# A hand-written order of 821 operations, written anew from the first product to the last chunk but one: linear attention into a SiLU layer on one Trainium2 core

## The chip, the cores and the metric

The kernel runs on one core of a Trainium2 chip. The core has TensorE (matrix products, in the profile PE, and PEld for its weight loads), VectorE (DVE), ScalarE (ACT), GpSimd (POOL) and SyncE (SP); 16 DMA engines move data between the device memory and the core's SBUF. Products land in PSUM, which has 8 banks. The metric is the device time of one execution in microseconds.

## The reference

Inputs `q`, `k`, `v` are 8 batches x 8 heads x 576 rows x 64; the two weight matrices are 512 x 2048 and 2048 x 512, all float32.

```python
q_s = exp(q - max(q, -1)); q_s /= sum(q_s, -1)          # over the 64 of a head
k_s = exp(k - max(k, 2));  k_s /= sum(k_s, 2)           # over the 576 rows
kv  = einsum('bhsd,bhse->bhde', k_s, v)                 # 64 x 64 per head
x   = einsum('bhsd,bhde->bhse', q_s, kv)                # then (4608, 512)
h   = x @ w_in
out = (h / (1 + exp(-h))) @ w_out                       # (4608, 512)
```

## The kernel before

The 4608 rows are worked as chunks 0 to 8. Chunk 0 is the 576 rows of batch 0; chunk 1 has 448 rows, chunks 2 to 8 have 512, and a chunk's rows may come from two batches. The attention of batch b is made just ahead of the chunks that need it.

The two layers of chunks 1 to 8 use a scheme with seven block products for eight (Strassen's, in Winograd's form): of rows, columns and inner dimension two halves each. It needs sums of weight blocks (once), of input blocks and of results. All names that follow are operations of the kernel; t is a chunk, b a batch, c one of two pairs of heads, i a product from 1 to 7.

- **Loads.** `lq`, `lk`, `lv` (b.c) load float32 halves of a batch, 576 KB each, into tiles with two buffers per name. Batch 0 and batches 3 to 7 are loaded by SyncE's queue, batches 1 and 2 by GpSimd's. `W1a0` to `W1d` (first layer) and `W2a` to `W2d` (second layer) are loaded by GpSimd's queue, which also turns them to float16.
- **Attention.** `eq`, `ek`: exp on ScalarE. `z`: row sums and reciprocal on VectorE. `n`: the division of q on GpSimd (line 216; batch 0 and `n1.1` on VectorE). `vc`: the cast of v to bfloat16, on GpSimd from batch 2 on (line 144). `tq`: one DMA transpose of q on SyncE's queue (line 226; batches 0 and 1 on TensorE, `tr`, with copies `tc`). `kv`, `kc`: the 64 x 64 products and their normalisation. `X`: the product that makes the layer's input, copied out of PSUM by `x` (suffix a: ScalarE, v: VectorE).
- **First layer.** Chunk 0, plainly: `w` is one block of 128 columns over 576 rows (8 matmuls of 288 columns), into one of four pairs of PSUM banks; `h` its tanh (ScalarE), `v` the product of it on VectorE. Chunk 1 does half of its columns plainly (`m`, with SiLU `mu`). The rest is done in two groups of seven products: `g t.group.i`, 8 matmuls each, lines 412 to 433. Products 1, 6, 7, 4 add up in banks 0 and 1; between them `s` copies the sum reached (to tiles h0, h1, h2), `a` adds products 2, 5, 3 to the copy (VectorE, line 403), and `u` applies SiLU (ScalarE, line 409). So product 6 must wait for the copy after product 1, product 7 for the copy after 6, and so on.
- **Second layer.** Chunk 0 plainly: `p`, with copies `po` and stores `os`. From chunk 1 on `b t.i.half` (8 matmuls, line 503), snapshots `sa`, `sb`, `sc`, sums `wa`, `wb`, `wc`, `wl` and stores `o t.half` (four DMAs on SyncE's queue). `o t.0` stores what `wa` and `wb` have filled.
- **Sums of SBUF operands on VectorE.** `WS group.i` (line 373) and `T i` (line 487) are sums of weight blocks, `xs` (line 383) of the layer's input, `S t.i` (line 477) of the first layer's results. `T1` needs the parts of the second layer's weights up to `W2b2`, `T2` all of them.
- `gcopy` copies the 64 rows of chunk 0's result that belong with chunk 1.

Nothing schedules the program. The body first writes out the head (lines 545 to 621: warm-up matmuls `heat`, batch 0's attention, the issue of the weight loads, the first halves of `w0` and `w2`). Then each operation is entered in a table under its name (lines 624 to 805), and the text `ORDER` (lines 18 to 67) lists the names; they are called in that order (lines 807 and 808), and each engine runs its own operations in the order in which they were called. Semaphores make an operation wait for the data it reads and for the buffers it overwrites, and whatever stands behind it on its engine waits with it. A DMA waits in its queue in the same way; the queue of GpSimd also holds GpSimd's operations.

Of the kernel before, what the change touches and what calls it, by code (L numbers as in the profile page):

```python
# [15 lines left out]


ORDER = """
    lk1.0 w1 lk1.1 w2 h1 w0 h2 v1 w3 h0 W2b1 w5 v0 v2 h3 w4 WS0.1 h5 w6 v3 h4 W2b2 v4 w7 v5 w8 h7 h6 v7 w9
    lv1.0 h8 v6 w11 v8 h9 lv1.1 w10 eq1.0.0 v9 h11 WS0.2 w12 eq1.1.0 v11 h10 w13 WS1.1 eq1.0.1 v10 h12 w15  # L20
    qp1a h13 v12 w14 eq1.1.1 v13 qp1b WS1.2 W2c1 p0 h14 z1.0 ek1.0 p1 z1.1.0 n1.0 z1.1.1 p2 h15 ek1.1 v15 p3
    WS1.4 W2c2 tr1.0 v14 lq2.0 p4 tc1.0a tc1.0b lq2.1 n1.1 p5 W2d p6 lk2.0 T1 vc1.0 lk2.1 p7 tr1.1 lv2.0
    vc1.1a vc1.1b gcopy WS1.3 kv1 lv2.1 tc1.1b p8 tc1.1a kc1 WS0.3 xt1.0 xt1.1 x1.0a x1.1v p9 x1.2a x1.3v
    g1.1.1 xs1.1 xs1.2 xs1.4 g1.1.2 s1.1.0a WS0.4 p10 xs1.3 eq2.0 a1.1.0 p11 eq2.1 z2.0 g1.1.6 g1.1.5
    s1.1.1a z2.1 n2.0 p12 ek2.0 g1.1.7 p13 s1.1.2v n2.1 ek2.1 p14 a1.1.2 g1.1.4 p15 tq2 u1.1.4 g1.1.3 po2v
    vc2.1 po1a m0 po3v po0a a1.1.1 u1.1.0 vc2.0 m1 lk3.0 mu0 m2 T2 lq3.0 mu1 lq3.1 m3 u1.1.2 lk3.1 T3 m4
    lv3.0 u1.1.1 lv3.1 m5 T4 mu2 os0 mu4 kv2 mu5 m6 mu3 kc2 X2.0 mu6 X2.1 x2.0v m7 x2.1a x2.3a x2.2v g2.1.1
    mu7 xs2.1 xs2.2 g2.1.2 s2.1.0v b1.1.0 ek3.0 S1.1 g2.1.6 eq3.1 lk4.0 S1.2 b1.2.0 os1 s2.1.1a b1.1.1 xs2.3
    xs2.4 eq3.0 a2.1.0 g2.1.7 vc3.0 sa1 b1.2.1 lq4.0 z3.1 s2.1.2a g2.1.5 vc3.1 ek3.1 b1.6.0 a2.1.2 n3.1
    lk4.1 g2.1.4 z3.0 g2.1.3 u2.1.0 g2.0.2 u2.1.4 wa1 n3.0 b1.6.1 a2.1.1 u2.1.2 g2.0.1 sb1 S1.3 kv3 tq3  # L30
    s2.0.0a b1.5.0 kc3 u2.1.1 S1.4 g2.0.6 b1.7.0 s2.0.1v lv4.0 ek4.1 b1.7.1 lv4.1 a2.0.0 os3 g2.0.7 sc1
    ek4.0 b1.5.1 s2.0.2v g2.0.5 eq4.0 lk5.0 wc1 lq4.1 g2.0.4 a2.0.2 os2 b1.4.0 vc4.0 lk5.1 z4.0 u2.0.4
    g2.0.3 u2.0.2 b1.3.0 lv5.0 vc4.1 a2.0.1 u2.0.0 lq5.0 b1.4.1 n4.0 X3.0 wl1v X3.1 kv4 x3.0a x3.1v x3.2a
    b1.3.1 kc4 x3.3a xs3.1 u2.0.1 g3.1.1 xs3.2 wb1 g3.1.2 s3.1.0a xs3.3 xs3.4 g3.0.2 S2.1 g3.1.6 S2.2 eq4.1
    b2.2.0 s3.1.1a b2.1.0 z4.1 ek5.0 b2.1.1 a3.1.0 g3.1.7 n4.1 sa2 ek5.1 b2.6.0 s3.1.2v g3.1.5 vc5.0 tq4
    g3.1.4 a3.1.2 u3.1.0 b2.6.1 u3.1.4 S2.3 g3.1.3 sb2 lq5.1 g3.0.1 u3.1.2 a3.1.1 lv5.1 lk6.0 b2.7.0 s3.0.0a
    o1.0 S2.4 b2.2.1 u3.1.1 a3.0.0 g3.0.6 lv6.0 b2.7.1 s3.0.1v eq5.0 g3.0.5 wa2 g3.0.7 sc2 lq6.0 z5.0 b2.4.0
    s3.0.2a lk6.1 b2.5.0 vc5.1 eq5.1 a3.0.2 g3.0.4 o1.1 n5.0 z5.1 g3.0.3 u3.0.4 b2.5.1 a3.0.1 n5.1 u3.0.0
    b2.4.1 wc2 u3.0.2 X4.0 X4.1 kv5 x4.1v x4.0a tq5 wl2v b2.3.0 u3.0.1 x4.3v g4.1.1 xs4.1 x4.2a b2.3.1 xs4.2
    s4.1.0a S3.1 g4.1.2 wb2 g4.1.6 lq6.1 a4.1.0 ek6.1 b3.1.0 xs4.3 s4.1.1a b3.1.1 xs4.4 S3.2 ek6.0 g4.1.5  # L40
    g4.1.7 sa3 eq6.0 b3.2.0 s4.1.2v eq6.1 b3.2.1 lq7.0 kc5 lk7.0 b3.6.0 a4.1.2 lv6.1 lq7.1 g4.1.4 o2.0 wa3
    g4.1.3 z6.0 u4.1.4 b3.5.0 u4.1.0 S3.3 g4.0.1 lk7.1 b3.6.1 a4.1.1 s4.0.0a g4.0.2 sb3 u4.1.1 g4.0.6 a4.0.0
    b3.5.1 s4.0.1a S3.4 b3.7.0 vc6.1 u4.1.2 g4.0.7 z6.1 vc6.0 g4.0.5 s4.0.2a b3.7.1 a4.0.2 n6.1 g4.0.4 sc3
    u4.0.2 g4.0.3 wc3 n6.0 b3.3.0 u4.0.4 a4.0.1 b3.4.0 u4.0.0 X5.0 X5.1 kv6 x5.0a x5.1v tq6 x5.3a x5.2v
    b3.3.1 u4.0.1 xs5.1 g5.1.1 xs5.2 wb3 b3.4.1 s5.1.0v o2.1 ek7.1 g5.1.2 kc6 g5.1.6 wl3a xs5.3 xs5.4 a5.1.0
    lv7.0 b4.2.0 s5.1.1a lv7.1 b4.1.0 S4.1 eq7.1 g5.1.7 ek7.0 b4.2.1 s5.1.2v o3.1 g5.1.5 S4.2 b4.1.1 u5.1.0
    a5.1.2 g5.1.4 sa4 g5.0.2 o3.0 u5.1.4 wa4 g5.1.3 S4.3 u5.1.2 vc7.1 g5.0.1 b4.6.0 a5.1.1 vc7.0 s5.0.0a
    b4.6.1 a5.0.0 u5.1.1 g5.0.6 S4.4 b4.5.0 s5.0.1a b4.5.1 sb4 u5.0.0 g5.0.7 g5.0.5 s5.0.2v b4.7.0 eq7.0
    a5.0.2 b4.7.1 z7.1 g5.0.4 sc4 g5.0.3 b4.4.0 a5.0.1 u5.0.4 b4.4.1 wc4 u5.0.1 X6.0 X6.1 kv7 x6.0v u5.0.2
# [17 lines left out]
"""


# [1 line left out]
def kernel(  # L71
# [477 lines left out]
    for name, src in (("qt", q), ("kt", k)):  # L549
        load(0, name, src, 0, nc.sync)  # L550
        if name == "qt":
            load(0, name, src, 1, nc.sync)
    load(0, "vt", v, 0, nc.sync)
    load(0, "kt", k, 1, nc.sync)
    load(0, "vt", v, 1, nc.sync)
# [283 lines left out]
```

## Time and profile before

| | us |
|---|---|
| median of 3 runs (256.9, 257.86, 258.57) | 257.86 |
| the profiled execution | 258.61 |
| its span, first to last instruction | 256.6 |
| TensorE busy in it | 249.1 |
| VectorE busy | 206.2 |
| ScalarE busy | 190.9 |
| GpSimd busy | 65.8 |

The span is shorter than the execution's own time by 2.0 us. A row of the profile's groups or of its timeline names a line of the kernel, an engine, an operation, what it writes and reads, how often, and how long; in brackets stands how long the engine had been idle and what ended that. The chain of work that ended last is followed back from the last instruction, at each step to what released it. Matmuls overlap each other, so the duration of one says little; the distance between starts says how fast they go.

The granted clock of TensorE is 1.00 of full speed in every window of the trace that was read.

### The profile page before, as it was taken

What the parts mean: (1) busy time and instruction counts of PE and PEld (TensorE: products, weight loads), DVE (VectorE), ACT (ScalarE), POOL (GpSimd) and SP (SyncE); (2) the same over time, 40 slices, a digit from 0 to 9 for tenths busy, and PEclk for the clock granted to TensorE, in tenths of its full rate; (3) what the DMA queues carried; (4) which work ended last, traced back from release to release, by engine and by line L of the source; (5) the groups of instructions that cost most, each with busy time, mean ns of one, the idle gap of its engine ahead of it and who ended that gap; (6) DMA issues with size and microseconds to landing.
All of it is one profiled execution on the core that took longest, in us unless ns stands there. A gap on an engine that the chain in (4) does not pass through costs nothing.

```text
span 256.6 us, 6459 instructions
## 1 busy us (share of the span) xinstructions
PE 249.1 (97%) x2732; PEld 204.2 (80%) x2732; DVE 206.2 (80%) x276; ACT 190.9 (74%) x225; POOL 65.8 (26%) x62
## 2 busy tenths in 40 slices
...
GB/s 248 348 181 297 302 301 283 351 140 393 378 128 213 403 187 137 361 335 168 276 266 68 224 236 3 3 52 32 163 14 153 13 0 4 148 18 0 66 141 123
DMA packets 36044, 45.89 MB, mean 179 GB/s; under 512 B 16288, under 2 KB 21088, under 8 KB 36016
## 3 DMA queue, kind: packets, MB, share of 16 engines
...
q10 hardware_dynamic: 400, 0.33, 0.6%
...
## 4 chain that ended last, share of the span: by engine, by line
PE 76%; DMA 11%; issue 5%; POOL 3%; ACT 2%; DVE 1%; ACTq 0%; POOLq 0%
PE PS L503 37%; PE PS L425 33%; DMA qt<-in_q_dram 5%; DMA kt<-in_k_dram 5%; PE PS L335 3%; PE PS L248 2%; PE PS L282 2%; POOL W L564 1%; DMA out_dram<-ow 1%; POOL qt L152 1%; DVE GT L323 1%; ACT L409 0%; POOL W L570 0%; ACT sg L320 0%; ACT GT L409 0%
## 5 line engine op out<-in xcount | busy, mean ns | idle before, releaser
L403 DVE TENSOR_TENSOR h<-PS,h 128x1024 f32<-128x1024 f32 (+1 forms) x45 | 54.2, 1206 | 9.3 <-PE PS L425 7.8
L503 PEld LDWEIGHTS <-GT 128*128 128x128 f16 x512 | 50.1, 98 | 5.9
L425 PEld LDWEIGHTS <-WS 128*128 128x128 f16 x480 | 46.7, 98 | 6.5 <-issue 0.6
L409 ACT ACTIVATE GT<-h 128x1024 f16<-128x1024 f32 (+1 forms) x45 | 46.8, 1051 | 0.9 <-DVE h L403 0.7
L503 PE MATMUL PS<-W,GT 128*128 128x256 f16 x384 | 47.3, 273 | 0.0
L425 PE MATMUL PS<-XS,WS 128*128 128x256 f16 (+1 forms) x360 | 45.0, 272 | 0.0
L142 ACT COPY h<-PS 128x1024 f32<-128x1024 f32 (+1 forms) x31 | 31.1, 1003 | 16.9 <-PE PS L425 15.7
L503 PEld LDWEIGHTS <-S 128*128 128x128 f16 x384 | 37.1, 98 | 4.6
L425 PEld LDWEIGHTS <-W 128*128 128x128 f16 x360 | 35.2, 98 | 4.4
L216 POOL TENSOR_TENSOR eq<-eq,rzq 128x1152 bf16<-128x1152 bf16 x13 | 27.3, 2115 | 37.6 <-DVE rzq L211 36.3
L503 PE MATMUL PS<-T,S 128*128 128x256 f16 x256 | 32.2, 273 | 0.0
L144 POOL CAST vaug<-vt 128x1152 bf16<-128x1152 f32 x12 | 15.8, 1328 | 61.5 <-DMA vt<-in_v_dram 61.4
L425 PE MATMUL PS<-XT,W 128*128 128x256 f16 (+1 forms) x240 | 29.7, 272 | 0.0
L144 DVE COPY h<-PS 128x1024 f32<-128x1024 f32 (+1 forms) x14 | 17.0, 1212 | 9.2 <-PE PS L425 4.4
L207 DVE TENSOR_REDUCE zq<-eq 128x18 f32<-128x1152 bf16 x14 | 18.8, 1342 | 4.1 <-ACT eq L163 4.0
L163 ACT ACTIVATE eq<-qt 128x1152 bf16<-128x1152 f32 (+1 forms) x18 | 18.9, 1055 | 3.1 <-DMA qt<-in_q_dram 2.8
L168 ACT ACTIVATE ek<-kt 128x1152 bf16<-128x1152 f32 x16 | 18.6, 1163 | 3.0 <-DMA kt<-in_k_dram 2.9
L791 POOL DMA_DIRECT2D out_dram<-ow x5 | 2.7, 545 | 70.0 <-DVE ow L773 70.0
L409 ACT ACTIVATE GT<-PS 128x1024 f16<-128x1024 f32 (+1 forms) x15 | 15.2, 1013 | 6.1 <-PE PS L425 6.1
L503 PE MATMUL PS<-T,GT 128*128 128x256 f16 x128 | 16.3, 272 | 0.0
L307 PE MATMUL PS<-XT,W 128*128 128x288 f16 x128 | 16.0, 286 | 0.2 <-DMA W<-in_moe_w_in_dram 0.2
L503 PE MATMUL PS<-W,S 128*128 128x256 f16 x128 | 16.1, 273 | 0.0
...
## 6 DMA issues: line engine op xcount, KB each, us to landing
...
```

The lines of the kernel that those rows point to most:

```text
L142: eng.copy(out=o, in_=i)
L144: eng.tensor_copy(o, i)
L163: nc.scalar.activation(out=half(st[b]["eq"], cc)[:, :, g0:g1], in_=jgd(b, "qt", cc)[:, :, g0:g1], func=ACT.Exp)
L168: nc.scalar.activation(out=half(ek, cc), in_=jgd(b, "kt", cc), func=ACT.Exp)
L207: nc.vector.reduce_sum(out=z, in_=e, axis=AX.X)
L216: eng.tensor_tensor(out=e, in0=e, in1=r[:, :, :, None].to_broadcast([128, J, 2, D]), op=ALU.mult)
L307: nc.tensor.matmul(out=PS[:, WIDE[fb] + n, 0:S // 2], lhsT=W1[:, c, fb * 128:(fb + 1) * 128], rhs=XTS[0][:, c, n * (S // 2):(n + 1) * (S / ...
L335: nc.tensor.matmul(out=PS[:, bank, o0:TCH], lhsT=W1[:, c, fb * 128:(fb + 1) * 128], rhs=XTS[t % 2][:, c, o0:TCH], start=(c == 0), stop=(c ...
L403: nc.vector.tensor_tensor(out=four(t, i), in0=group_bank(t, g), in1=four(t, i), op=ALU.add)
L409: nc.scalar.activation(out=group_out(t, f, n), in_=x, func=ACT.Silu, scale=1.0 / XS)
L425: nc.tensor.matmul(out=PS[:, bank + p // 2, (p % 2) * HT:(p % 2) * HT + width(t)], lhsT=a[:, c, p * 128:(p + 1) * 128], rhs=bb[:, c, 0:wid ...
L503: nc.tensor.matmul(out=PS[:, bank, m * HN:(m + 1) * HN], lhsT=a[:, fc, m * 128:(m + 1) * 128], rhs=bb[:, fc, :], start=(first and fc == 0) ...
```

## The change

The head becomes operations with names of their own, each `w` becomes two operations (`w.0`: inner blocks 0 and 1, `w.1`: blocks 2 and 3), and the list is written anew from its beginning to the end of chunk 8's first group. From `g8.0.2` on it is the old one, and so is the order of SyncE's transfers. The new list keeps positions in which VectorE's sums of SBUF operands and GpSimd's operations do not stand side by side; there is no wait that would enforce it. No operation is added or taken away. The places that the prediction speaks of, first the old list, then the new one:

```diff
-    lk1.0 w1 lk1.1 w2 h1 w0 h2 v1 w3 h0 W2b1 w5 v0 v2 h3 w4 WS0.1 h5 w6 v3 h4 W2b2 v4 w7 v5 w8 h7 h6 v7 w9
...
-    lv1.0 h8 v6 w11 v8 h9 lv1.1 w10 eq1.0.0 v9 h11 WS0.2 w12 eq1.1.0 v11 h10 w13 WS1.1 eq1.0.1 v10 h12 w15
-    qp1a h13 v12 w14 eq1.1.1 v13 qp1b WS1.2 W2c1 p0 h14 z1.0 ek1.0 p1 z1.1.0 n1.0 z1.1.1 p2 h15 ek1.1 v15 p3
-    WS1.4 W2c2 tr1.0 v14 lq2.0 p4 tc1.0a tc1.0b lq2.1 n1.1 p5 W2d p6 lk2.0 T1 vc1.0 lk2.1 p7 tr1.1 lv2.0
-    vc1.1a vc1.1b gcopy WS1.3 kv1 lv2.1 tc1.1b p8 tc1.1a kc1 WS0.3 xt1.0 xt1.1 x1.0a x1.1v p9 x1.2a x1.3v
-    g1.1.1 xs1.1 xs1.2 xs1.4 g1.1.2 s1.1.0a WS0.4 p10 xs1.3 eq2.0 a1.1.0 p11 eq2.1 z2.0 g1.1.6 g1.1.5
-    s1.1.1a z2.1 n2.0 p12 ek2.0 g1.1.7 p13 s1.1.2v n2.1 ek2.1 p14 a1.1.2 g1.1.4 p15 tq2 u1.1.4 g1.1.3 po2v
-    vc2.1 po1a m0 po3v po0a a1.1.1 u1.1.0 vc2.0 m1 lk3.0 mu0 m2 T2 lq3.0 mu1 lq3.1 m3 u1.1.2 lk3.1 T3 m4
-    lv3.0 u1.1.1 lv3.1 m5 T4 mu2 os0 mu4 kv2 mu5 m6 mu3 kc2 X2.0 mu6 X2.1 x2.0v m7 x2.1a x2.3a x2.2v g2.1.1
...
-    g4.1.3 z6.0 u4.1.4 b3.5.0 u4.1.0 S3.3 g4.0.1 lk7.1 b3.6.1 a4.1.1 s4.0.0a g4.0.2 sb3 u4.1.1 g4.0.6 a4.0.0
-    b3.5.1 s4.0.1a S3.4 b3.7.0 vc6.1 u4.1.2 g4.0.7 z6.1 vc6.0 g4.0.5 s4.0.2a b3.7.1 a4.0.2 n6.1 g4.0.4 sc3
...
-    x6.3v b4.3.0 x6.1a kc7 b4.3.1 x6.2a xs6.1 xs6.2 g6.1.1 xs6.4 wl4v g6.1.2 S5.1 s6.1.0a b5.1.0 a6.1.0
-    g6.1.6 xs6.3 g6.0.2 wb4 s6.1.1a S5.2 b5.1.1 o4.0 b5.2.0 S5.3 g6.1.7 S5.4 b5.2.1 s6.1.2a z7.0 g6.1.5 sa5
-    g6.1.4 wa5 n7.0 b5.6.0 a6.1.2 u6.1.4 b5.6.1 g6.0.1 n7.1 sb5 u6.1.0 g6.1.3 s6.0.0a b5.7.0 a6.1.1 tq7
-    b5.7.1 a6.0.0 u6.1.1 g6.0.6 sc5 b5.5.0 s6.0.1a o4.1 g6.0.5 u6.1.2 g6.0.7 b5.5.1 s6.0.2v b5.4.0 wc5
-    g6.0.4 a6.0.2 b5.4.1 u6.0.4 b5.3.0 u6.0.2 X7.0 X7.1 x7.0a x7.1v g6.0.3 x7.2a xs7.1 u6.0.0 g7.1.1 x7.3v
...
+    kc0.1 heat3 x0.0a x0.0v X0.1 w0.0 x0.1a w2.0 x0.1v w1.0 w0.1 w1.1 w2.1 h0 h1 WS0.1 w3.0 lk1.1 w3.1 v0 h2 v1 v2
+    h3 w4.0 v3 w5.0 w4.1 w6.0 h4 w5.1 w7.0 W2b1 h5 v4 w7.1 w6.1 w8.0 v5 w8.1 WS0.2 lk1.0 h7 w9.0 v7 w9.1 h6 w11.0 v6
+    W2b2 w11.1 w10.0 lv1.0 w10.1 h8 h9 WS0.3 eq1.0.0 v8 v9 h11 w12.0 w13.0 v11 eq1.0.1 h10 w12.1 w13.1 w15.0 v10
+    w14.0 qp1a lv1.1 w14.1 WS1.1 qp1b eq1.1.0 w15.1 h13 W2c1 v13 h12 v12 p0 p1 WS1.2 h15 p2 z1.0 p3 v15 p4 p5 h14
+    eq1.1.1 ek1.0 z1.1.0 v14 p6 W2c2 ek1.1 n1.0 z1.1.1 tr1.0 p7 WS1.3 lq2.0 vc1.0 n1.1 tc1.0a tc1.0b tr1.1 vc1.1a
+    lq2.1 vc1.1b kv1 lk2.0 tc1.1a tc1.1b kc1 p8 xt1.0 xt1.1 p9 x1.0a W2d x1.2a WS1.4 x1.1v g1.1.1 xs1.1 x1.3v g1.1.2
+    xs1.2 eq2.0 p10 s1.1.0a g1.1.6 xs1.3 z2.0 eq2.1 lk2.1 lv2.1 p11 s1.1.1a a1.1.0 z2.1 lv2.0 n2.0 n2.1 g1.1.5
+    g1.1.7 xs1.4 p12 ek2.0 gcopy s1.1.2v a1.1.2 ek2.1 vc2.1 tq2 p13 vc2.0 g1.1.4 T1 g1.1.3 T2 u1.1.4 p14 p15 lk3.0
+    po0a po1a a1.1.1 u1.1.0 m0 m1 WS0.4 mu0 m3 mu1 T4 u1.1.1 T3 m4 m2 po3v m5 kv2 lq3.0 po2v u1.1.2 mu2 mu5 mu4 kc2
+    mu3 m6 X2.0 X2.1 mu6 x2.0v m7 x2.1a xs2.1 x2.2v lq3.1 x2.3a xs2.2 g2.1.1 lk3.1 mu7 ek3.0 s2.1.0v eq3.1 b1.1.0
...
+    g4.1.3 g4.0.1 sb3 u4.1.0 b3.5.0 o2.0 s4.0.0a a4.1.1 b3.5.1 g4.0.6 b3.7.0 X5.1 u4.1.1 s4.0.1a z6.1 g4.0.7 u4.1.2
...
+    s6.1.1a z7.1 b5.1.1 g6.1.7 S5.1 xs6.4 g6.1.5 s6.1.2a a6.1.2 o3.0 u6.1.0 b4.3.0 g6.1.4 sa5 g6.1.3 u6.1.4 b4.3.1
+    S5.2 g6.0.1 a6.1.1 n7.1 b5.6.1 s6.0.0a u6.1.1 S5.3 b5.6.0 wb4 g6.0.6 sb5 b5.2.0 b5.2.1 s6.0.1a a6.0.0 g6.0.7
+    b5.7.0 g6.0.5 b5.7.1 u6.1.2 s6.0.2v g6.0.4 u6.0.0 a6.0.2 g6.0.3 sc5 o4.0 u6.0.4 b5.4.0 S5.4 wa5 tq7 X7.1 o4.1
+    X7.0 a6.0.1 x7.3v x7.1v u6.0.2 b5.4.1 x7.2a x7.0a xs7.1 g7.0.2 g7.1.1 u6.0.1 wl5a xs7.2 s7.1.0a b6.1.0 g7.1.2
...
     for fb in range(NFB):
-        op(f"w{fb}", wide_mm, fb, range(2 if fb in (0, 2) else 0, NC))
+        op(f"w{fb}.0", wide_mm, fb, (0, 1))
+        op(f"w{fb}.1", wide_mm, fb, (2, 3))
```

The rest of the diff moves the head's calls, unchanged in kind and in their engines, into the table (for instance `op("W2a", load_w2, 0, 4)`).

More of the change, by code (lines that the diff above doesn't have):

```diff
@@ L29 @@
[L29 to L33, printed above, removed]
@@ new lines @@
+    lq4.1 vc4.1 u2.0.1 S2.1 xs3.1 wb1 xs3.2 s3.1.0a b2.1.0 os2 xs3.4 S2.2 b2.1.1 b2.2.0 eq4.1 lk5.1 xs3.3 b2.2.1 sa2
+    g3.1.6 s3.1.1a z4.1 g3.1.2 kv4 g3.1.7 lv5.0 a3.1.0 g3.1.5 s3.1.2v ek5.0 b2.6.1 a3.1.2 u3.1.0 g3.1.4 b2.6.0
+    u3.1.4 lq5.0 S2.3 n4.0 g3.1.3 kc4 g3.0.1 n4.1 sb2 g3.0.2 tq4 u3.1.2 b2.7.0 a3.1.1 s3.0.0a a3.0.0 lq5.1 wa2
+    g3.0.6 u3.1.1 lv5.1 lk6.0 o1.0 b2.7.1 s3.0.1v g3.0.5 eq5.0 vc5.0 S2.4 vc5.1 z5.0 sc2 g3.0.7 b2.4.0 s3.0.2a
+    b2.5.0 g3.0.4 lv6.0 b2.5.1 a3.0.2 eq5.1 g3.0.3 z5.1 ek5.1 b2.4.1 wc2 b2.3.0 u3.0.4 n5.0 X4.0 u3.0.2 X4.1 a3.0.1
@@ new lines @@
+    b3.4.1 X5.0 a4.0.1 n6.0 kv6 g5.1.2 wl3a x5.0a lk7.1 u4.0.2 x5.1v g5.1.1 tq6 u4.0.1 xs5.1 kc6 g5.0.2 b4.1.0 xs5.2
+    o2.1 s5.1.0v ek7.0 g5.1.6 b4.1.1 b3.3.0 s5.1.1a sa4 xs5.3 a5.1.0 g5.1.7 S4.1 b3.3.1 eq7.0 S4.2 g5.1.5 xs5.4
+    u5.1.0 s5.1.2v g5.1.4 b4.6.0 lv7.0 wb3 u5.1.4 a5.1.2 g5.1.3 z7.0 g5.0.1 b4.2.0 a5.1.1 s5.0.0a b4.2.1 wa4 a5.0.0
+    u5.1.1 lv7.1 S4.3 g5.0.6 u5.1.2 b4.6.1 s5.0.1a b4.5.0 g5.0.7 sb4 b4.7.1 g5.0.5 b4.7.0 eq7.1 s5.0.2v n7.0 ek7.1
+    vc7.0 a5.0.2 S4.4 g5.0.4 vc7.1 sc4 u5.0.4 g5.0.3 u5.0.2 b4.4.0 u5.0.0 b4.4.1 a5.0.1 X6.1 X6.0 x6.1a x6.0v kv7
@@ new lines @@
+    xs8.4 b7.2.0 S7.2 b7.2.1 a8.1.2 o6.0 g8.1.4 o6.1 u8.1.0 g8.1.3 u8.1.4 S7.3 g8.0.2 a8.1.1 u8.1.2 g8.0.1 u8.1.1
+    b7.6.0 s8.0.0v b7.6.1 wa7 g8.0.6 a8.0.0 sb7 b7.5.0 s8.0.1a S7.4 b7.7.0 g8.0.7 g8.0.5 s8.0.2v b7.7.1 a8.0.2
+    b7.5.1 sc7 u8.0.0 g8.0.4 wc7 g8.0.3 u8.0.4 b7.4.0 a8.0.1 u8.0.2 b7.3.0 u8.0.1 b7.3.1 e1.0 wb7 S8.1b e1.1 o7.0
+    S8.1a b7.4.1 S8.2a sa8 S8.2b e2.0 wl7v e6.0 S8.3 o7.1 e6.1 e2.1 sb8 e5.0 waE0 S8.4 qa00g qa01s e7.0 waE1 e7.1
+    qa11g qa10a e5.1 sc8 wcE0 e3.0 wcE1 qc01g wxE0 qc11a e3.1 wbE0 qc00a wxE1 qb00g qb01s e4.0 wbE1 qc10s qb10g e4.1
@@ L67 @@
+    qb11s wlE0a ql01a ql00s wlE1a ql11a ql10s
 """
@@ L548 @@
     make_identity(nc, ident_f)
[L549 to L555, printed above, removed]
     nc.vector.tensor_copy(ident, ident_f)
```

115 lines of the change are left out of this document (42 added, 73 removed).

## The prediction

> **What bounds the kernel now.** I read the engine sums first, then the chain that ended last, then TensorE's product starts, then the engines' timelines where TensorE loses time.
>
> ```profile
> span 256.6 us, 6459 instructions
> PE 249.1 (97%) x2732; PEld 204.2 (80%) x2732; DVE 206.2 (80%) x276; ACT 190.9 (74%) x225; POOL 65.8 (26%) x62
> ```
>
> TensorE (PE) is nearly always busy, but a matmul's 273 ns overlap its neighbours, so the share may hide gaps. The chain gives the spacing:
>
> ```profile
> 50.73 1.14 issue
> 51.87 1.28 ACT L409
> ...
> 53.16 0.93 ACT GT L409
> ...
> 54.13 4.70 PE PS L335 x24
> ...
> 148.12 3.49 PE PS L425 x32
> 151.62 1.75 PE PS L503 x16
> ...
> 237.22 11.37 PE PS L503 x104
> ```
>
> From 54.13 us to the last product the chain stays on TensorE, and 3.49 us over 32 matmuls is 109 ns each, here and in the rows around it. "Trace Analysis" ("Identifying the Most-Contended Engine") of the Trainium skill warns that matmul busy time misjudges TensorE because matmuls are pipelined; here the spacing, not the 97%, carries the claim.
>
> So I took from the trace when each product starts and how far it is to the next, against the shortest distance of its kind: 0.98 us for a block of the first layer of chunk 0 (w), 0.86 for one of its second layer (p), 0.77 and 0.75 for a product (g1) and a plain block (m) of chunk 1, 0.87 for a later product (g, b). From the first w at 14.96 to the end of chunk 7's products the excess is 2.1 us before 54.13 (0.37 at w1, 0.28 at p3, 0.46 at g1.1.5, 0.76 before m0, 0.27 in small ones) and 1.7 us after it, in pieces of about 0.1 us, mostly where the matmul's shape changes. That is the most that any order can win in the stretch that this change touches: 3.8 us, of which about 2.3 us (2.1 and two pieces in chunk 1) look like waits.
>
> **The change, part by part.** It removes and adds no instruction: the built programs hold the same instructions on every engine (2732 matmuls, 16 activation-table loads of 1.28 us, the same DMAs), and no wait between VectorE and GpSimd is added. The four parts are where order can matter.
>
> *VectorE's sums and GpSimd.* What overlap costs now, from the timeline:
>
> ```profile
> 54.20 3.26 POOL L144 CAST vaug<-vt 128x1152 bf16<-128x1152 f32 x2 [2.54 <-DMA vt<-in_v_dram]
> 54.79 1.65 DVE L487 TENSOR_TENSOR T<-W,T 128x2048 f16<-128x2048 f16 x1
> ...
> 56.36 2.17 DVE L487 TENSOR_TENSOR W<-W 128x2048 f16<-128x2048 f16 x1
> ...
> 58.45 1.21 DVE L487 TENSOR_TENSOR T<-W,T 128x2048 f16<-128x2048 f16 x1
> ```
>
> The same operation takes 1.21 us alone and 1.65 or 2.17 beside a GpSimd cast; the second cast takes 2.15 for 1.16. "SBUF — State Buffer" ("Who interferes with whom") of the Trainium skill says that a VectorE operation with two SBUF inputs and a GpSimd operation that reads SBUF exclude each other, the later one waiting for all of the earlier; the trace agrees (a cast ending at 57.46 plus 1.21 gives 58.67, measured 58.52). Over the kernel the lengthened sums are T3 0.96, S1.3 0.59, T2 0.44 and WS1.2 0.21: 2.2 us of VectorE's 206, and about 2 us of GpSimd. The chain above has neither engine on it there, since TensorE has other products to run. I cost it at nothing; the bounds are -2.2 us (each second late at TensorE) and 0. If the order drifts and sums and casts still meet, the same cover holds.
>
> *First layer (14.96 to 31).* w1 now waits 0.37 us in its middle, until 16.51 (second quarter of W1, issued 9.48, 7.0 us to landing). The new order runs three first halves before it (3 x 0.49 = 1.47, to 16.43) instead of two: up to -0.3. The next weights, issued 10.23 and 8.9 us under way, land at 19.1, where w4.0 would come at 19.0: +0.1. Net -0.2. VectorE keeps up: v12 and v13 end near 31.1 and 30.5, and p0's first two matmuls need v13 alone. Bounds -0.3 and +0.4 (p0 held whole until v12).
>
> *Second layer and attention of batch 1 (31 to 54).* p3's 0.28 goes, since tr1.0 now stands behind p6 and n1.0 ends at 34.69. Next late: vc1.1a. ScalarE had vc1.0 at 36.56 (1.16) and vc1.1a until 38.69; now tc1.0a (0.68) is between: 36.56 + 1.16 + 0.68 + 0.67 = 39.1, so kv1 at 39.15 for 39.31. Up to m0 the end is set elsewhere: m0 needs u1.1.4, behind a table load and ek2.1, which waits for the load of k that lands at 50.61. GpSimd's queue issues the same bytes ahead of it (W2d only swaps with lk2.0), so 50.61 stays, and with it m0 at 54.13. The second-layer product p12 now waits for W2d until about 49.1 (47.6 now), but then p12, p13, g1.1.4, g1.1.3, p14, p15 (4 x 0.86 + 2 x 0.77) end at 54.1. So 0. Bounds: this queue lost about 1.7 us between 41.9 and 47.6, when one slice of 0.5 us moved 140 GB/s and later ones near 400; without that, ek2.1 comes earlier and products alone reach m0 at 53.3: -0.8. I take 0, the row as it is.
>
> *Chunk 1 to the first product of chunk 2 (54 to 62).* p15 now directly precedes m0, so its copy po0a cannot start before 54.3 where po1a started at 53.98. ScalarE then runs po0a to x2.1a, thirteen operations, back to back: +0.3 at g2.1.1. VectorE gets T1 and WS0.4 (1.21 + 0.68) here from before 45 us: after a1.1.2, near 51, T1, T2, a1.1.1, WS0.4, T4, T3 and two copies sum to 8 us at uncontended rows and 8.8 with one cast met, to 59 or 59.8; kc2 must wait for kv2 at 59.6 anyway. Bounds 0 and +0.8.
>
> *Chunks 2 to 7.* I compared, for each product that waits for an evacuation, the TensorE work between it and the product evacuated with the evacuating engine's work. Before, there were at least two products (1.75 us) for one copy or add of 1.0 to 1.2 us. After, one place falls short: g4.0.6 to g4.0.7 has 0.87 + 0.23 us for s4.0.1a, 1.01 plus some 0.3 from the product's last start to the copy and back (g1.1.1 and u1.1.4 show 0.25 and 0.05): +0.2. At g7.0.2 x7.3v falls short by +0.1. Loads, table loads and sums keep their places within one or two products. Bounds 0 and +0.6.
>
> **Sum:** -0.2 + 0 + 0.2 (0 at m0 swallows the gains before it, so the first two count as 0) + 0.3 + 0.3 = **+0.6 us** on the profiled execution, which took 258.61 us, 256.6 of it span. That execution is 0.75 above the median of the runs shown (257.86), so I predict 257.86 + 0.6 = 258.46, say **258.4 us**. From the bounds: -0.8 to +1.8.
>
> **Rivals.**
> *TensorE's waits all go.* If the k load lands early and ScalarE keeps pace, the 2.3 us go: 256.2 executed, 255.5 as a median, -0.9%. For: all four large waits are in the reordered stretch. Against: the one before m0 hangs on bytes that are not reordered in total. 0.08.
> *VectorE is the bound after all* (the rule on the shared port, worked out): 92 to 96% busy from 64 to 115 us; each second of the 2.2 comes back, 255.7. Against: no product waited there. 0.04.
> *Slower: the last transpose comes late.*
>
> ```profile
> 170.47 2.39 SPq L441 DMA_DIRECT2D out_dram<-ow  x4
> 179.87 2.71 SPq L226 DMA_TRANSPOSE qT<-eq  x1
> ```
>
> SyncE's order is unchanged: the four stores of o4.0 stand ahead of tq7. They ended at 172.86; in the new order wb4, which fills what they store, stands behind b4.3.1, a6.1.1 and S5.3, near 176.0. Stores 2.4 (this row) to 3.7 (o3.0's), then the transpose's 4.6 to 6.3 us to landing, give 183.0 to 186.0. X7.1, moved 3.9 us forward, wants it at 185.0 (188.9 before). So it decides from wb4 at 175.0 to 177.9 on; by the worst rows TensorE waits 1.0 us, and each microsecond that wb4 slips adds one. With wb4 one to two later: 259.5 to 261.5. 0.14.
> *It doesn't do what it says:* sums and casts still meet, because only positions changed. Then some sums keep 1.6 to 2.2 us, and the time is that of the forecast; inside it.
>
> **How the numbers follow.** Forecast 0.72, gains 0.08 and 0.04, slower 0.14, 0.02 for what I don't see. The runs shown spread by 1.7 us, so a median moves by some 0.7. Range: -0.8 - 0.8 on 257.86 gives 256.3; above, +1.8 + 0.7, and half of the slower rival, give 260.7. Under 1% (2.6 us) this kernel's measurement hardly tells a change. Faster by over 1% needs more than all of TensorE's waits: 0.04. Slower: 0.13. Same: 0.83.
>
> **What would show it.** m0 near 54.1 with ek2.1 waiting for k; g2.1.1 near 62.0; g4.0.7 0.2 us late; no sum over 1.3 us if the separation works; X7.1 without a wait for the transpose, products at 109 ns per matmul to the end. I am wrong if chunks 2 to 7 show a wait over 0.5 us, if m0 moves by over 1 us, or if the order makes a load late (ScalarE waiting for q or k).

## The result and the profile after

| | before | after |
|---|---|---|
| median, us | 257.68 | 260.61 |
| range of its runs | 256.9 to 258.57 | 259.9 to 261.91 |
| ratio, 95% interval | | 1.0125 [1.0099, 1.0151] |
| the profiled execution | 258.61 | 261.91 |
| its span | 256.6 | 260.1 |
| VectorE busy | 206.2 | 210.3 |
| the last product (e4.1) starts at | 251.91 | 255.43 |

The change costs 2.9 us; 258.4 was forecast, and 260.61 lies just inside the range of 256.3 to 260.7. The engine sums on the page of the profile after, whose columns are busy time, share of the span and instructions:

```profile
span 260.1 us, 6458 instructions
PE 250.6 (96%) x2732; PEld 204.3 (79%) x2732; DVE 210.3 (81%) x276; ACT 191.5 (74%) x225; POOL 65.5 (25%) x62
```

VectorE executes the same 276 instructions in 4.1 us more. The operations have become longer. Where that matters is told by the chain that ended last, which in the old order stays on TensorE from 54.13 us on. The chain of the profile after (start, length, what):

```profile
50.92 2.11 DVE T L487
...
53.06 2.05 DVE T L487
...
60.31 0.30 DVE kvn L261
...
60.65 0.47 PE PS L282 x8
61.12 0.70 DVE XT L144
...
66.08 1.29 DVE XS L383
67.36 1.14 DVE h L403
68.50 1.75 DVE S L477
...
71.80 1.17 DVE h L403
72.97 0.04 issue
73.01 1.03 PE PS L425 x8
```

For 22 us, from 50.92 to 73.01, VectorE sets the end, but for 0.5 us of TensorE at 60.65. The three longest idle times of TensorE between 54 and 180 us, from the view of the waits of the profile after (who waited for whom; us in total, times, longest):

```profile
PE PS L425 <- DVE h L403: 1.1, 1, 1.1
PE PS L425 <- DVE XS L383: 1.0, 1, 1.0
PE PS L282 <- DVE kvn L261: 0.6, 1, 0.6
```

By the distance between product starts, as the prediction measured them, these are: **0.83 us** at the first X2 (its two halves lie 1.07 us apart, 0.24 in the old order; it waits for kc2, the rows named kvn), **1.22** ahead of g2.1.3 (waits for the add a2.1.2) and **1.20** ahead of g6.1.4 (waits for the sum xs6.4), with 0.26 more behind that one at g6.1.3. Together 3.5 us, and e4.1 starts 3.5 us later than before. What else moved cancels out: m0 starts at 53.55 for 54.13, pieces of about 0.1 us take that back.

VectorE's rows at these three places, from the timeline of the profile after (start, length, engine, line, operation, what it writes and reads):

```profile
50.92 2.10 DVE L487 TENSOR_TENSOR T<-W 128x2048 f16<-128x2048 f16 x1
53.06 2.05 DVE L487 TENSOR_TENSOR T<-W,T 128x2048 f16<-128x2048 f16 x1
...
65.99 1.37 DVE L383 TENSOR_TENSOR XS<-XT 128x512 f16<-128x512 f16 x1
...
68.42 1.83 DVE L477 TENSOR_TENSOR S<-S,GT 128x2048 f16<-128x2048 f16 x1
...
171.77 1.16 DVE L477 TENSOR_TENSOR S<-GT 128x2048 f16<-128x2048 f16 x1
172.85 2.33 DVE L383 TENSOR_TENSOR XS<-XT,XS 128x512 f16<-128x512 f16 x1
```

In order these are T1, T2, xs2.3, S1.2, S5.1 and xs6.4. Elsewhere in the same trace a T or an S takes 1.21 us and an xs 0.42. GpSimd's rows beside them, from the same view (in brackets its idle time and what ended it):

```profile
50.79 1.16 POOL L144 CAST vaug<-vt 128x1152 bf16<-128x1152 f32 x1
52.19 1.85 POOL L144 CAST vaug<-vt 128x1152 bf16<-128x1152 f32 x1 [0.24 <-DMA vt<-in_v_dram]
65.67 1.42 POOL L144 CAST vaug<-vt 128x1152 bf16<-128x1152 f32 x1 [11.63 <-DMA vt<-in_v_dram]
68.02 1.16 POOL L144 CAST vaug<-vt 128x1152 bf16<-128x1152 f32 x1 [0.92 <-DMA vt<-in_v_dram]
...
172.00 2.90 POOL L216 TENSOR_TENSOR eq<-eq,rzq 128x1152 bf16<-128x1152 bf16 x1 [15.26 <-DVE rzq L211]
```

So the new order, which is said to keep VectorE's sums and GpSimd's operations apart, has more of them together than the old one: about 6 us of lengthening on VectorE (the five long rows above, S1.3 and S4.3), against 2.2. The brackets tell why. The last row is n7.1. The list has it behind a6.1.1, an add that starts at 177.4 us; n7.1 started at 172.00, as soon as the row sums z7.1 were there, after 15 us in which GpSimd had been idle. vc3.0 and vc3.1 are listed behind z3.0 (72.9 us); they started at 65.67 and 68.02, when their loads landed. An engine runs its own operations in listed order, but the list does not tie its operations to those of another engine.

"SBUF — State Buffer" ("Who interferes with whom") of the Trainium skill adds that the order in which the two are issued decides which is blocked, not their shapes. The rows agree: n7.1 began while S5.1 ran and ended 1.97 us after S5.1's end (172.93), about its length of 2.12 alone; xs6.4, next in line on VectorE, ended at 175.18, 0.28 us after n7.1.

### The profile page after: what moved, and what is told of

Read it like the earlier page. It is cut to its first block, busy times and chain, and to the rows that moved or that the text cites. A ratio compares the mean times of both kernels' runs of the same rounds, so it can differ in the third digit from the quotient of the medians.

```text
span 260.1 us, 6458 instructions
## 1 busy us (share of the span) xinstructions
PE 250.6 (96%) x2732; PEld 204.3 (79%) x2732; DVE 210.3 (81%) x276; ACT 191.5 (74%) x225; POOL 65.5 (25%) x62
## 4 chain that ended last, share of the span: by engine, by line
PE 72%; DVE 12%; DMA 8%; issue 5%; ACT 1%; POOL 1%; ACTq 0%; DVEq 0%; POOLq 0%
PE PS L503 33%; PE PS L425 28%; PE PS L307 5%; DMA vt<-in_v_dram 4%; DMA W<-in_moe_w_in_dram 4%; PE PS L445 3%; DVE h L403 2%; DVE T L487 2%; DVE S L477 2%; PE PS L282 2%; DVE XS L383 1%; PE PS L248 1%; DVE XT L144 1%; DVE zq L207 1%; DMA out_dram<-ow 1%
## 5 line engine op out<-in xcount | busy, mean ns | idle before, releaser
L503 PE MATMUL PS<-W,GT 128*128 128x256 f16 x384 | 48.0, 273 | 0.0
L216 POOL TENSOR_TENSOR eq<-eq,rzq 128x1152 bf16<-128x1152 bf16 x13 | 28.2, 2176 | 46.4 <-DVE rzq L211 39.7
L144 POOL CAST vaug<-vt 128x1152 bf16<-128x1152 f32 x12 | 14.8, 1239 | 47.8 <-DMA vt<-in_v_dram 38.1
L425 PE MATMUL PS<-XT,WS 128*128 128x256 f16 (+1 forms) x120 | 15.4, 272 | 1.1 <-DVE h L403 1.1
L425 PE MATMUL PS<-XS,W 128*128 128x256 f16 (+1 forms) x120 | 15.4, 272 | 1.0 <-DVE XS L383 1.0
```

The lines of the kernel that those rows point to most:

```text
L144: eng.tensor_copy(o, i)
L216: eng.tensor_tensor(out=e, in0=e, in1=r[:, :, :, None].to_broadcast([128, J, 2, D]), op=ALU.mult)
L425: nc.tensor.matmul(out=PS[:, bank + p // 2, (p % 2) * HT:(p % 2) * HT + width(t)], lhsT=a[:, c, p * 128:(p + 1) * 128], rhs=bb[:, c, 0:wid ...
L503: nc.tensor.matmul(out=PS[:, bank, m * HN:(m + 1) * HN], lhsT=a[:, fc, m * 128:(m + 1) * 128], rhs=bb[:, fc, :], start=(first and fc == 0) ...
```

## The experiments

**Theory A:** GpSimd's operations start by their data and not by their places in the list, and in the new order they meet sums directly ahead of what TensorE waits for next. **Theory B:** the meetings are as harmless as before, and the order itself leaves VectorE too little time ahead of these products.

All ratios are to the kernel before, run beside it on the same chip. The last columns are TensorE's waits behind 54 us in the profiled execution, in us; the last row has earlier losses.

| kernel | median | ratio, interval | X2.0 | g2.1.3 | g6.1.4, g6.1.3 | elsewhere |
|---|---|---|---|---|---|---|
| after, GpSimd's work cut | 257.61 | 1.0018 [1.0008, 1.0028] | 0 | 0 | 0 | |
| before, GpSimd's work cut | 257.06 | 1.0002 [0.9988, 1.0015] | 0 | 0 | 0 | |
| after, xs6.4 first | 259.20 | 1.0083 [1.0055, 1.0110] | 0.85 | 1.41 | 0 | |
| after, vc3 behind n3.1 | 262.09 | 1.0187 [1.0170, 1.0204] | 0.82 | 0 | 1.46 | g2.0.7 0.9, X3.0 1.2 |
| after, again | 259.85 | 1.0119 [1.0099, 1.0140] | 0.88 | 0.60 | 1.46 | |
| after, n7.1 held | 258.58 | 1.0059 [1.0034, 1.0084] | 0 | 0 | 0 | |
| before, a meeting put in | 260.11 | 1.0109 [1.0092, 1.0126] | 0 | 0 | 1.62, 1.28 | |
| after, four operations moved | 259.34 | 1.0090 [1.0074, 1.0106] | 0 | 0 | 0 | b1.7.0 1.6 |
| after, T1 early | 259.46 | 1.0087 [1.0067, 1.0106] | 0 | 0.73 | 1.46 | |
| after, T1 early and xs6.4 first | 257.79 | 1.0026 [1.0016, 1.0037] | 0 | 0 | 0 | |
| before, with the new first layer | 258.67 | 1.0079 [1.0048, 1.0111] | 0 | 0 | 0 | tr1.0 2.4; p4 to p6 1.7, at half clock |

### GpSimd's divisions and casts cut, in both kernels

```diff
+        n = 1 if eng is nc.gpsimd else J
-        e = half(st[b]["eq"], cc)
-        r = st[b]["rzq"][:, cc]
+        e = half(st[b]["eq"], cc)[:, 0:n]
+        r = st[b]["rzq"][:, cc, 0:n]
...
+        if eng is nc.gpsimd:
+            o, i = o[:, 0:1], i[:, 0:1]
         copy(eng, o, i)
```

In the new order:

> The changed kernel with GpSimd's divisions of q (n, batches 1 to 7) and casts of v (vc, from batch 2 on) cut to one of their nine row blocks: 8/9 of these two are left out, every operation keeps its place, its waits and its readers. Theory A (in the new order sums and GpSimd's operations meet at places where TensorE waits next for VectorE: T1 and T2 before the first X2, xs2.3 and S1.2 before a2.1.2, xs6.4 before g6.1.4): the sums return to 1.21 and 0.42 us, TensorE's waits of 0.83 (X2.0), 1.22 (g2.1.3) and 1.20 + 0.26 us (g6.1.4, g6.1.3) go, the time falls by 2.5 to 3.5 us, to 257 to 258. Theory B (the new order itself leaves too little VectorE time ahead of those products, with or without GpSimd): the three waits stay above half their size and the time stays within 1 us of 260.6.

In the old one:

> The same cut in the kernel before: 8/9 of GpSimd's divisions of q (batches 1 to 7) and casts of v (from batch 2 on) are left out. Both theories: the sums lengthened there (T3, S1.3, T2, WS1.2, 2.2 us together) return to their short times, but TensorE does not wait for them, so the time stays within 0.7 us of the kernel before. If it falls by 1.5 us or more, meeting sums cost the old order too, and A does not tell the two kernels apart.

Measured: the new order fell from 1.0125 to 1.0018, that is by 2.7 us, and no wait of TensorE from 54 to 200 us is left in its trace. VectorE's timeline of the new order without this work has T1 and T2 short:

```profile
50.28 1.21 DVE L490 TENSOR_TENSOR T<-W 128x2048 f16<-128x2048 f16 x1
51.53 1.22 DVE L490 TENSOR_TENSOR T<-W,T 128x2048 f16<-128x2048 f16 x1
```

The old order did not move (1.0002). This is A: the length of GpSimd's work is what the new order pays for, and the old order does not pay for it. What stays of the new order without it is 0.2% or 0.5 us. From m0 to the last product this trace takes 198.28 us and that of the old order with the same cut 197.78. Of the 0.50 us, 0.45 lie in the distances from the kv and X operations to what follows them, in pieces of about 0.1 us; the new list has other products behind them. Why the distances are longer there was not tested.

### One sum moved out of the way

```diff
-    s6.1.1a z7.1 b5.1.1 g6.1.7 S5.1 xs6.4 g6.1.5
+    s6.1.1a xs6.4 z7.1 b5.1.1 g6.1.7 S5.1 g6.1.5
```

> The changed kernel with one sum, xs6.4 (0.42 us), moved on VectorE from behind z7.1 and S5.1 to directly ahead of z7.1. Nothing else moves. A: xs6.4 runs before n7.1 can start, takes 0.42 us for 2.33, and g6.1.4 and g6.1.3 no longer wait: -1.2 to -1.5 us, about 259.3; n7.1 then meets S5.1 alone, for which no product waits. B: g6.1.4 waits for ScalarE's and VectorE's other work all the same: 0 to -0.4 us.

Measured: 259.20 us. xs6.4 took 0.41 us, n7.1 still started right behind z7.1 (172.12) and met S5.1 alone, and the 1.46 us at g6.1.4 and g6.1.3 are gone. The two other waits were there (1.41 us at g2.1.3), and the ratio fell by about 1 us, a little less than the 1.2 to 1.5 of A.

### Two casts moved out of the way

```diff
-    g2.1.4 z3.1 a2.1.2 z3.0 vc3.0 g2.1.3 b1.6.1 u2.1.4 u2.1.0 vc3.1 g2.0.1 wa1 n3.1
+    g2.1.4 z3.1 a2.1.2 z3.0 g2.1.3 b1.6.1 u2.1.4 u2.1.0 g2.0.1 wa1 n3.1 vc3.0 vc3.1
```

> The changed kernel with GpSimd's two casts vc3.0 and vc3.1 listed behind n3.1 instead of ahead of it, so that GpSimd's own order holds them until n3.1 has its row sums (72 us or a little earlier). VectorE's order is untouched. A: xs2.3 takes 0.42 us for 1.37 and S1.2 1.21 for 1.83, a2.1.2 ends 1.5 us earlier and the 1.22 us wait of g2.1.3 goes: -1.0 to -1.3 us, unless the transpose behind n3.0 (about 78.5 for 76.8 us) makes the first X3 late, which would show as a wait there of up to 0.7 us. B: VectorE works without a pause from 62 to 74 us, so a2.1.2 stays late: 0 to -0.3 us.

Measured: slower than the changed kernel, 1.0187. The local part came as A has it: xs2.3 took 0.42 us, S1.2 1.22, and g2.1.3 did not wait. But the division n3.0 now stood behind the two casts and met the next sums. One row of VectorE's timeline of this kernel (its lines are numbered one lower):

```profile
75.40 3.13 DVE L476 TENSOR_TENSOR S<-GT,S 128x2048 f16<-128x2048 f16 x1
```

And GpSimd's timeline of the same kernel:

```profile
74.37 3.09 POOL L215 TENSOR_TENSOR eq<-eq,rzq 128x1152 bf16<-128x1152 bf16 x1
```

n3.0 waited for S1.3 (until 75.4) and S1.4 then for n3.0. The copy s2.0.1v behind S1.4 came late, and g2.0.7 waited 0.9 us for it. X3.0 waited 1.2 us for ScalarE, and a row of ScalarE's timeline says why ScalarE was late:

```profile
82.20 1.16 ACT L162 ACTIVATE eq<-qt 128x1152 bf16<-128x1152 f32 x1 [2.28 <-DMA qT<-eq]
```

This is eq4.0, which overwrites the tile that the transpose tq3 reads, and tq3 stands behind n3.0. So the transpose did make X3.0 late, as the exception in A's text has it, but by way of ScalarE and by 1.2 us for 0.7. The meeting of n3.0 with S1.3 and S1.4 had been overlooked: in this stretch a sum that TensorE soon needs stood at the later place of GpSimd's work too.

### The changed kernel again, and GpSimd held at its listed place

> The changed kernel itself, to stand beside the others on one chip and to see which of its waits come back. A: the waits of 0.8 us at the first X2, 1.2 to 1.4 at g2.1.3 and 1.2 + 0.26 at g6.1.4 and g6.1.3 are there again, since list, data and durations fix them; the 0.73 us wait at w4.0 may be smaller, since it hangs on one weight load (0 to 0.46 us in the three runs so far). 260 to 260.7 us, 1.0 to 1.4% above the kernel before. B expects the same.

The waits came back, the one at g2.1.3 with half its size (0.60): here S1.2 took 1.21 us for 1.83, and the cast vc3.1 beside it 2.23 for 1.16. The hold is one added element ahead of n7.1:

```diff
-    S5.2 g6.0.1 a6.1.1 n7.1 b5.6.1
+    S5.2 g6.0.1 a6.1.1 hold71 n7.1 b5.6.1
...
+    op("hold71", lambda: nc.gpsimd.tensor_copy(gate, H[1][0:1, 0:1]))
```

> The changed kernel with one element added ahead of n7.1 on GpSimd: a copy of a single number out of the tile that a6.1.1 writes, so that n7.1 cannot start before a6.1.1, the place at which the list has it. Nothing else is changed; VectorE's order is that of the changed kernel, xs6.4 behind S5.1 included. A (list places do not hold GpSimd): n7.1 starts near 177 us instead of 172.0, S5.1 and xs6.4 take 1.2 and 0.42 us, g6.1.4 and g6.1.3 do not wait, -1.2 to -1.5 us; n7.1 then meets S5.2 or S5.3, for which no product waits. B: the order of VectorE's work (z7.1, S5.1, xs6.4) makes g6.1.4 late by itself, 1.6 + 1.2 us stand ahead of the sum: its wait stays above 0.8 us.

GpSimd's rows in the timeline of this kernel:

```profile
174.47 1.11 POOL L778 COPY gate<-h 1x1 f32<-1x1 f32 x1 [20.53 <-DVE h L402]
175.54 2.11 POOL L215 TENSOR_TENSOR eq<-eq,rzq 128x1152 bf16<-128x1152 bf16 x1
```

And VectorE's, with S5.1 and xs6.4 in the changed kernel's order:

```profile
168.96 1.16 DVE L476 TENSOR_TENSOR S<-GT 128x2048 f16<-128x2048 f16 x1
170.04 0.41 DVE L382 TENSOR_TENSOR XS<-XT,XS 128x512 f16<-128x512 f16 x1
```

xs6.4 takes 0.41 us for 2.33, behind z7.1 and S5.1 as in the changed kernel, and g6.1.4 does not wait: it was not VectorE's order but n7.1 in it, as A says. The median is 1.3 us lower than that of the changed kernel beside it. In this one profiled execution the other two waits are missing too. The hold, which stands over 100 us later, cannot cause that, so not all of the 1.3 us need be its own. What stands there instead is new. T1 started at 50.30 us and the cast vc2.1 at 50.37, and T1 took 1.22 us. In four profiles of the changed kernel or of one that is the same up to there, the cast started 0.07 to 0.14 us ahead of T1, and T1 took 2.09 to 2.16. Which starts first by a tenth of a microsecond decides over 0.9 us.

### A meeting put into the old order

```diff
-    b5.1.1 o4.0 b5.2.0 S5.3 g6.1.7 S5.4 b5.2.1 s6.1.2a z7.0 g6.1.5
+    b5.1.1 o4.0 b5.2.0 z7.0 S5.3 xs6.4 g6.1.7 S5.4 b5.2.1 s6.1.2a g6.1.5
```

(xs6.4 stood behind g6.1.1 in the old list.)

> The kernel before with the meeting put in: z7.0 moved ahead of S5.3 on VectorE, and xs6.4 behind S5.3, so that n7.0 starts on GpSimd while S5.3 runs and xs6.4 comes behind both. By the durations alone, xs6.4 then ends near 174.8 on the time axis of its profile, 0.2 to 0.4 us later than g6.1.4 wants it. A: n7.0 waits for S5.3, xs6.4 for n7.0 (2.1 us), and ends near 176.7: g6.1.4 waits 1.8 to 2.5 us and the time rises by as much, to 259 to 259.5. B: +0.2 to +0.5 us.

Measured: +3.2 us by the medians and +2.8 by the ratio, more than A's 1.8 to 2.5. VectorE's timeline of this kernel:

```profile
171.44 1.16 DVE L473 TENSOR_TENSOR GT<-GT 128x2048 f16<-128x2048 f16 x1
172.52 2.33 DVE L379 TENSOR_TENSOR XS<-XT,XS 128x512 f16<-128x512 f16 x1
174.77 3.13 DVE L473 TENSOR_TENSOR S<-GT,S 128x2048 f16<-128x2048 f16 x1
```

And its waits of TensorE between 165 and 185 us:

```profile
PE PS L421 <- DVE XS L379: 1.5, 1, 1.5
PE PS L421 <- DVE h L399: 1.1, 1, 1.1
```

The first wait is the expected one, 1.62 us by the starts. The second is that of the sum behind: n7.1 follows n7.0 on GpSimd without a pause, S5.4 waits for it as xs6.4 did for n7.0 (3.13 us for 1.22), and the add a6.1.2 behind S5.4 makes g6.1.3 1.28 us late. Two operations of VectorE in other places cost the old kernel about as much as the whole change does.

### Repairs: sums moved, GpSimd's work whole

Four moves at once:

```diff
-    n1.1 tc1.0a
+    n1.1 T1 tc1.0a
...
-    g1.1.4 T1 g1.1.3 T2
+    g1.1.4 g1.1.3 T2
...
-    g2.1.4 z3.1 a2.1.2 z3.0
+    g2.1.4 a2.1.2 z3.1 z3.0
...
-    b1.7.0 S1.4 kv3 b1.7.1 s2.0.1v g2.0.7 lv4.0 a2.0.0
+    b1.7.0 kv3 b1.7.1 s2.0.1v g2.0.7 lv4.0 a2.0.0 S1.4
...
-    s6.1.1a z7.1 b5.1.1 g6.1.7 S5.1 xs6.4 g6.1.5
+    s6.1.1a xs6.4 z7.1 b5.1.1 g6.1.7 S5.1 g6.1.5
```

> The changed kernel with four operations of VectorE moved: xs6.4 ahead of z7.1, T1 behind n1.1 (from 50.9 to about 37.5 us, before the casts of v of batch 2), z3.1 behind a2.1.2 and S1.4 behind a2.0.0. GpSimd's operations and their places are untouched. A: the waits at the first X2, g2.1.3 and g6.1.4 go (-0.5, -1.2, -1.4 us; kv1 may come 0.3 later for T1), and 257.3 to 258.3 us remain, the time of the kernel with GpSimd's work cut; wherever a sum still meets GpSimd's work, as S1.3 does n3.0, no product waits for it. B: VectorE's load in the stretch from 48 to 80 us is the same, so most of the first two waits comes back later, at g2.0.7 or the first X3: above 259 us.

Measured: 259.34, which is B's figure (above 259). The three waits are gone, but a new one came, and the last sentence of A's expectation was wrong. z3.1 and z3.0 are now neighbours, so n3.1 and n3.0 run from 71.42 to 75.6 without a pause, and S1.3 stands in the middle. VectorE's timeline of this kernel, a2.1.2 and S1.3:

```profile
68.44 1.23 DVE L402 TENSOR_TENSOR h<-PS,h 128x1024 f32<-128x1024 f32 x1 [1.49 <-PE PS L424]
...
74.39 2.31 DVE L476 TENSOR_TENSOR GT<-GT 128x2048 f16<-128x2048 f16 x1
```

b1.7.0, which reads what S1.3 writes, could have started at 75.15 and started at 76.76, 1.6 us late. Not all of that is the meeting. Where z3.1 stayed ahead of a2.1.2 (the last kernel of this section) it fills the idle time that the first row has in brackets, and S1.3 starts at 72.80, 1.6 us earlier than here. An estimate from these rows: with 1.21 us S1.3 would have ended near 75.6, so about 0.5 us belong to the place of z3.1, which is VectorE's order and nearer to B, and about 1.1 to the meeting.

Then T1 alone (the first two parts of this diff):

> The changed kernel with T1 alone moved, from behind a1.1.2 (50.9 us) to directly behind n1.1 (about 37 us), where GpSimd only issues loads. A, with what the profiles so far add: in six of seven profiles of this order the cast vc2.1 started about 0.1 us ahead of T1, and T1 took 2.1 us and T2 2.05; in one T1 started 0.07 us ahead of the cast and took 1.22, and there the waits at the first X2 and at g2.1.3 were both missing. So T1 out of the way saves 0.9 us of waiting and 1.2 us of work ahead of kc2, both waits go (the second because VectorE then has S1.2 behind it before the casts of v of batch 3 arrive), kv1 comes 0.1 to 0.3 later, g6.1.4's wait stays: 1.0 to 2.0 us below the changed kernel, 0.4 to 0.7% above the kernel before. B: the wait at g2.1.3 stays at 0.6 to 1.2 us, since the same work stands in front of it from the first X2 on: 0.5 to 0.9 us below the changed kernel.

(The count "six of seven" in this text is wrong: among the profiles with GpSimd's work whole it is four of five.) Measured: 1.0087, about 0.8 us below the changed kernel, less than A's 1.0. The wait at X2.0 went, that at g2.1.3 stayed with 0.73 us. Both are inside what B says; B's reason, that the same work stands in front of g2.1.3, is answered by the next kernel, which has that work and no wait. And T1 together with xs6.4 (the first two parts and the last):

> The changed kernel with two sums moved: T1 behind n1.1 and xs6.4 ahead of z7.1. A: none of the three waits is left although GpSimd's work is whole, and the time is that of the kernel with GpSimd's work cut, 256.9 to 257.9 us, within 0.3% of the kernel before. B: 258.5 us or more.

Measured: 257.79, and no wait of TensorE between 54 and 200 us. The two kernels have the same list up to 165 us, so the 0.73 us need another cause. In the first, the cast vc3.0 came first (GpSimd's timeline, T1 alone):

```profile
65.94 1.16 POOL L143 CAST vaug<-vt 128x1152 bf16<-128x1152 f32 x1 [12.62 <-DMA vt<-in_v_dram]
```

and S1.2 on VectorE 0.07 us behind it:

```profile
66.01 2.15 DVE L476 TENSOR_TENSOR S<-S,GT 128x2048 f16<-128x2048 f16 x1
```

In the second, TensorE and VectorE were 0.3 us earlier from the first layer on, S1.2 won and took 1.22 us (VectorE's timeline, T1 and xs6.4):

```profile
65.71 1.22 DVE L476 TENSOR_TENSOR S<-S,GT 128x2048 f16<-128x2048 f16 x1
```

with the cast at 65.96 waiting instead (1.99 us for 1.16). B's forecast for the pair, 258.5 or more, fell: with two sums moved, the new order with GpSimd's work whole is 0.26% above the old one. Neither this nor any other kernel of the study is faster than the kernel before, and the traces point to none: the old order has no meeting that TensorE notices.

### The first layer alone

```diff
...
+    w14.0 qp1a lv1.1 w14.1 WS1.1 qp1b eq1.1.0 w15.1 h13 W2c1 v13 h12 v12
+    eq1.1.1 WS1.2 p0 h14 z1.0 ek1.0 p1 z1.1.0 n1.0 z1.1.1 p2 h15 ek1.1 v15 p3
...
```

(the new list above, the old one from the second line on)

> The first part of the change alone: the new list up to the first product of the second layer (p0), and behind it the old list's order of everything that is left. A and B alike: the first layer loses 0.4 to 0.5 us at w3 or w4 in either order when one weight load is late and nothing when it is not, m0 waits for the load of k as before, so the time is that of the kernel before within 0.2% (-0.5 to +0.5 us), and what the change costs lies behind it. If it is 1 us or more slower, the first layer has a part in the loss that the waits counted so far do not show.

Measured: 1.0079, outside both expectations, and no answer on the first layer. p0 starts at 30.85 us (30.67 to 31.41 in the other profiles), so up to there nothing is lost. The loss is at the seam, 4.1 us in the profiled execution, which with 260.86 us was the slowest of its six. It has two parts. The first, 2.4 us, is a wait. The new list loads lk1.0 behind other loads, and the old one asks for it early. ScalarE's timeline of this kernel:

```profile
34.21 1.16 ACT L167 ACTIVATE ek<-kt 128x1152 bf16<-128x1152 f32 x1 [2.81 <-DMA kt<-in_k_dram]
35.28 0.63 ACT L319 ACTIVATE sg<-PS 128x576 f32<-128x576 f32 x1
```

The second row, h15, stands behind ek1.0 on ScalarE, and the product v15 behind it on VectorE. tr1.0, which overwrites the PSUM banks that v15 reads, waited for that (TensorE's timeline):

```profile
36.75 0.66 PE L233 MATMUL PS<-ident,eq 128*128 128x128 bf16 x9 [2.28 <-DVE GT L322]
```

The changed kernel has h15 ahead of ek1.0 and pays nothing here: the two parts of its list belong together. The second part, 1.7 us, is no wait: p4, p5 and p6 took 0.28, 0.84 and 0.57 us longer than a p elsewhere, while the granted clock of TensorE was 0.50 from 37.82 to 41.23 us. No other profile has such a stretch before its last product.

## Why the prediction was wrong

**The step that failed** is the first part, the sums and GpSimd: "I cost it at nothing; the bounds are -2.2 us (each second late at TensorE) and 0. If the order drifts and sums and casts still meet, the same cover holds." That they would still meet was foreseen, and even the rival "It doesn't do what it says" was named, but with "the time is that of the forecast". Both rest on the cover of the old order, which had been read from a chain that stays on TensorE. The new order has other sums at the meeting points, and the cover has to be worked out again there. With GpSimd's work cut to a ninth no product waits in either order; whole, it costs nothing measurable in the old and 2.7 us in the new. The upper bound should have been a loss: a sum of 0.42 us took up to 2.33, one of 1.21 up to 2.16 in the changed kernel and 3.13 in others, and what stands behind it on VectorE is late with it. Two of the prediction's own signs of being wrong came: waits over 0.5 us in chunks 2 to 7, and sums over 1.3 us.

**Chunk 1 to the first product of chunk 2 (+0.3, bounds 0 and +0.8)**: measured 0.83 us of waiting. g2.1.1 starts at 61.96, where "near 62.0" was forecast, but only because m0 was 0.58 us early. The term had VectorE's eight operations at "8 us at uncontended rows and 8.8 with one cast met"; both casts met both sums, and they took 9.2 (50.92 to 60.1). With GpSimd's work cut the wait is 0. ScalarE, on which I put the 0.3, shows no wait there.

**Chunks 2 to 7 (+0.3, bounds 0 and +0.6)**: measured 2.7 us, the two waits at g2.1.3 and g6.1.4. The comparison of each copy and add with TensorE's work between used 1.0 to 1.2 us for every one and left out what stands in front of them on VectorE. The two places named as short, g4.0.7 and g7.0.2, show 0.13 us and none.

**First layer (-0.2, bounds -0.3 and +0.4)**: within the bounds; p0 at 31.41 for 31.02. The wait at w1 went as worked out, the one at w4.0 was 0.73 us for 0.1. It hangs on one load (landed at 19.60 us) and not on the order: in ten profiles that share the new first layer it shows in three, with 0.46 to 0.73, and one of the three profiles of the old order has 0.53 at the same weights.

**Second layer and attention of batch 1 (0, bound -0.8)**: p3's 0.28 and g1.1.5's 0.46 are gone, 0.34 at g1.1.2 is new, kv1 came at 39.42 (39.15 was worked out). m0 starts at 53.55, since ek2.1, which waits for the load of k, starts at 49.28 for 50.69 and the products alone set m0, as the bound of -0.8 had it. But that row was itself the exception: in the two other profiles of the old order m0 starts at 52.93 and 52.63. The gain of 0.58 is one of the two executions, not of the orders.

**The slower rival** (the last transpose late) did not come. SyncE's queue in the profile after:

```profile
180.43 2.38 SPq L441 DMA_DIRECT2D out_dram<-ow  x4
182.92 2.84 SPq L226 DMA_TRANSPOSE qT<-eq  x1
```

The stores of o4.0 end at 182.8, later than the 179.7 that 176.0 and the longer store of 3.7 gave, and tq7 is issued 3.1 us later than in the old profile. But X7.1 had become late itself (189.56 for the 185.0 worked out) and did not wait. The pair of T1 and xs6.4 shows what the rival would have done without the other waits. Its wb4 starts at 175.53 (near 176.0 was worked out) and its X7.1 at 185.13, and SyncE's queue there has tq7 in time:

```profile
178.74 2.81 SPq L225 DMA_TRANSPOSE qT<-eq  x1
```

It lands 4.7 us after its issue, at 183.4, and X7.1 does not wait. The chance of 0.13 for slower stood on the wrong mechanism. That 260.61 lies inside the range is luck too: without the half of this rival its upper end is 257.86 + 1.8 + 0.7 = 260.4.

(In the rival without waits the sum is off by 0.1 us: 258.61 - 2.3 is 256.3. Nothing hangs on it.)

Not settled: why 0.2 to 0.3% are left with all three waits gone.
